# Whole-tile loads of k and v and a four-quadrant k-by-v product, in an attention and feed-forward kernel

## Chip, cores, metric

The kernel runs on one core of a Trainium2 chip. The metric is the device time of one execution in us; the trace of one profiled execution is read beside it. A ratio of two kernels is the mean time of one's fast runs over the mean of the other's fast runs of the same rounds, so it is not quite the ratio of the medians that are quoted.

In the profiles PE is TensorE, PEld its weight loads, DVE VectorE, ACT ScalarE, POOL GpSimd, and SP the engine whose queue issues most loads. The tiles kv_ps, o_ps, h_ and o_ hold k by v, q by kv, and the two large products. A kv section is an unbroken run of k-by-v matmuls. TensorE at half clock is TensorE at a granted clock of 0.50.

## The reference, cut

```python
kv  = np.einsum('bhsd,bhse->bhde', k, v)         # q, k, v: (8, 8, 576, 64) float32
out = np.einsum('bhsd,bhde->bhse', q, kv)
rms = np.sqrt(np.mean(out * out, axis=-1, keepdims=True) + 1e-06)
x   = (out / rms * g_norm).transpose(0, 2, 1, 3).reshape(4608, 512)
h   = x @ w_in                                    # 512 x 2048
y   = np.maximum(0.01 * h, h) @ w_out             # 2048 x 512
```

## The kernel before

The 4608 tokens are worked off in nine blocks of 512. Block 0 also rounds the weights, which arrive as float64, on ACT and DVE. Blocks 1 to 8 do the two large products by Strassen's scheme (tiles h_a to h_c and o_a to o_c). The attention of the next batch is cut into steps that are slipped between these products. The parts that the change touches, for batches 1 to 7:

```python
def load_rows(eng, src, t):                       # two heads, in two pieces of 64 rows
    pin(eng.dma_start(t[:64], src[:, :SLO, :].rearrange("h (p j) d -> p h j d", j=JJ)))   # j = 5
    pin(eng.dma_start(t[64:, :, :J], src[:, SLO:, :].rearrange("h (p j) d -> p h j d", j=J)))  # 4
...
def load_pair(b, p):                              # k, v, then q in four pieces, all on SP's queue
...
def attention_kv(b, p, kv_ps):                    # one pair of heads: two column tiles of 64
    k_in, v_in = k_ins.pop((b, p)), v_ins.pop((b, p))
    for j in range(JJ):
        n = P if j < J else 64
        for l in range(2):
            matmul(kv_ps[64 * l:64 * l + 64, p, :], lhsT=k_in[:n, l, j, :],
                   rhs=v_in[:n, l, j, :], start=(j == 0), stop=(j == JJ - 1))
...
def attention(b):
    ...
    for p in range(NP):                           # four pairs, one step each
        q_in = q_ins.pop((b, p))
        nc.vector.transpose(...)                  # q to qT
        attention_kv(b, p, kv_ps)
        nxt = (b, p + 2) if p + 2 < NP else (b + 1, p + 2 - NP)
        if nxt[0] < B:
            load_pair(*nxt)                       # k, v, q have two buffers each
        yield
    copy_kv(b, slice(0, NP), kv_ps)
    yield
    ...                                           # q by kv (o_ps), norm
```

Batch 0 has its own start: its loads go out first on two queues, TensorE transposes q, and "warm-keeping" matmuls on zeros (the program's name for them; the granted clock was 1.00 up to 29.95 us) stand between its sections, three of them between the four kv sections.

## Time and profile before

| | before |
|---|---|
| time, median of 4 runs of the first comparison | 1001.1 us |
| span of the profiled run | 996.7 us |
| first h_ps of block 0 | 31.35 us |
| start of block 1 (first h_a) | 158.84 us |
| first o_ps of batches 2, 3, 4, 7 | 185.3, 292.1, 397.8, 715.0 us |

The tables of this document give starts in us from the begin of the span. A row of a timeline has start, length, engine, line, operation, tiles, shape and count; the bracket gives idle time before it and what ended that. The prediction shows the rows of before.

### The profile page before, as it was taken

How to read it: one execution, taken by the hardware profiler on the slowest of the kernel's cores; microseconds unless marked ns; L12 is line 12 of the kernel's file. 1: busy time of each engine (PE TensorE's matmuls, PEld its weight loads, DVE VectorE, ACT ScalarE, POOL GpSimd, SP SyncE). 2: the span in 40 equal slices, each digit the busy share in tenths (PEclk: the TensorE clock that was granted, in tenths of full speed). 3: DMA queues.
4: the chain of work that ended last, by engine and by line, in shares of the span. 5: the costliest groups of instructions: out<-in, count | busy, mean ns of one | idle time of the engine just before them, and what ended most of it. 6: DMA issues, size and time to landing. Idle time of an engine off the chain costs nothing.

```text
span 996.7 us, 13085 instructions
## 1 busy us (share of the span) xinstructions
PE 970.3 (97%) x5130; PEld 766.5 (77%) x5130; DVE 435.6 (44%) x682; ACT 268.1 (27%) x531; POOL 500.7 (50%) x395
## 2 busy tenths in 40 slices
PE   9799999999999999999999999999999999999997
PEld 4444446778887888888887888788878888888885
DVE  1967993264235533363335433553246321422223
ACT  2644442431123211421133113311242122112210
POOL 1000213656655665556556665566556666666642
PEclk9799999999999999999999999999999999999999
DMA  9979904400340016000620043004100010001001
GB/s 208 224 177 246 232 15 117 115 2 0 95 137 1 1 52 178 2 1 0 175 58 1 1 128 103 2 0 95 43 1 1 1 43 1 1 1 43 0 1 43
DMA packets 45948, 63.41 MB, mean 64 GB/s; under 512 B 5952, under 2 KB 39744, under 8 KB 45888
## 3 DMA queue, kind: packets, MB, share of 16 engines
q1 hardware_dynamic: 35328, 51.96, 21.1%
q10 hardware_dynamic: 10432, 10.62, 3.4%
q8 instruction: 41, 0.67, 0.3%
q14 instruction: 19, 0.16, 0.1%
q0 software_dynamic: 128, 0.00, 0.0%
HBM read 53.12 MB, written 9.44 MB: 63 GB/s over the span
## 4 chain that ended last, share of the span: by engine, by line
PE 83%; DVE 4%; DMA 2%; SPq 1%; ACT 1%; issue 1%; DVEq 0%
PE o_a L87 21%; PE h_a L87 21%; PE h_c L87 11%; PE o_c L87 11%; PE o_b L87 6%; PE h_b L87 6%; PE o_acc L87 2%; PE kv_ps L87 2%; PE h_ps L87 2%; PE o_ps L87 2%; DVE qT L320 1%; DVE sum L282 1%; DMA v_in<-in_v_dram 1%; DMA k_in<-in_k_dram 1%; DVE g L388 0%
## 5 line engine op out<-in xcount | busy, mean ns | idle before, releaser
L388 DVE TENSOR_TENSOR o<-o_a,o 128x512 f32<-128x512 f32 x104 | 71.5, 688 | 132.8 <-PE o_a L87 132.8
L87 PE MATMUL o_a<-wt,gs 128*128 128x256 f32 x512 | 122.6, 382 | 0.0
L388 POOL TENSOR_TENSOR ws<-w 128x512 f32<-128x512 f32 x32 | 44.4, 1389 | 132.6 <-PE h_a L87 94.5
L388 POOL TENSOR_TENSOR wt<-w,w 128x512 f32<-128x512 f32 x32 | 40.9, 1280 | 139.0 <-PE o_a L87 135.6
L87 PEld LDWEIGHTS o_a<-wt,gs 128*128 128x128 f32 x512 | 95.9, 190 | 15.3 <-issue 1.9
L467 ACT ACTIVATE g<-g 128x512 f32<-128x512 f32 x96 | 60.5, 630 | 165.3 <-DVE g L388 165.3
L388 POOL TENSOR_TENSOR ws<-w,w 128x512 f32<-128x512 f32 x32 | 42.2, 1319 | 110.2 <-ACT cut L192 109.4
L388 POOL TENSOR_TENSOR gs<-g,g 128x512 f32<-128x512 f32 x64 | 81.5, 1274 | 22.9 <-ACT g L467 22.5
L472 ACT COPY g<-h_a 128x512 f32<-128x512 f32 x32 | 18.8, 586 | 251.0 <-PE h_a L87 239.1
L388 POOL TENSOR_TENSOR wt<-w,wt 128x512 f32<-128x512 f32 x64 | 83.9, 1310 | 2.5
L388 POOL TENSOR_TENSOR wt<-w 128x512 f32<-128x512 f32 x32 | 41.5, 1297 | 64.2 <-PE o_a L87 64.2
L87 PE MATMUL h_a<-xt,w 128*128 128x256 f32 x256 | 61.2, 382 | 7.8 <-DVE g L388 7.8
L87 PE MATMUL h_ps<-xT,w 128*128 128x512 f32 (+1 forms) x136 | 62.1, 605 | 6.6 <-DVE xT L301 4.5
L388 DVE TENSOR_TENSOR g<-h_b,g 128x512 f32<-128x512 f32 x32 | 22.1, 690 | 95.5 <-PE h_b L87 95.5
L388 DVE TENSOR_TENSOR o<-o_c,o 128x512 f32<-128x512 f32 x56 | 38.4, 685 | 56.8 <-PE o_c L87 56.8
L87 PE MATMUL o_a<-wt,g 128*128 128x256 f32 x256 | 60.8, 380 | 1.9 <-DVE o L388 1.9
L87 PE MATMUL h_a<-xT,ws 128*128 128x256 f32 x256 | 62.4, 386 | 0.0
L87 PE MATMUL h_a<-xt,ws 128*128 128x256 f32 x256 | 61.7, 384 | 0.0
L87 PE MATMUL o_a<-w,g 128*128 128x256 f32 x256 | 60.6, 379 | 0.8 <-DVE o L388 0.8
L87 PEld LDWEIGHTS h_a<-xt,w 128*128 128x128 f32 x256 | 48.1, 190 | 16.9 <-DVE g L388 10.6
L388 DVE TENSOR_TENSOR g<-h_c,g 128x512 f32<-128x512 f32 x32 | 22.1, 692 | 88.9 <-PE h_c L87 88.9
L87 PE MATMUL h_a<-xT,w 128*128 128x256 f32 x256 | 60.6, 379 | 0.0
(86 smaller groups left out, 1797.6 us busy)
## 6 DMA issues: line engine op xcount, KB each, us to landing
out_dram<-o ACTq DMA_DIRECT2D x36, 256.0 KB, 2.2
raw<-in_moe_w_in_dram SPq DMA_DIRECT2D x64, 128.0 KB, 5.0
raw<-in_moe_w_out_dram SPq DMA_DIRECT2D x16, 512.0 KB, 5.7
q_in<-in_q_dram SPq DMA_DIRECT2D x56, 144.0 KB, 3.5
q_in<-in_q_dram SPq DMA_DIRECT2D x56, 140.0 KB, 3.5
k_in<-in_k_dram SPq DMA_DIRECT2D x30, 160.0 KB, 3.7
v_in<-in_v_dram SPq DMA_DIRECT2D x30, 160.0 KB, 3.8
k_in<-in_k_dram SPq DMA_DIRECT2D x30, 128.0 KB, 3.7
```

What stands on the lines that cost most here:

```text
L87: pin(nc.tensor.matmul(*args, **kw))
L282: nc.vector.tensor_add(sums[l], sums[l], sq)
L320: nc.vector.transpose(qT[:, p, :].rearrange("p (t s) -> p s t", s=T), q_in.rearrange("p (s d) -> p s d", d=D)[:, :, :32])
L388: eng.tensor_tensor(out_, a, b_, op=ALU.subtract if minus else ALU.add)
L467: nc.scalar.activation(t, t if src is None else src, func=AF.Prelu, alpha=SLOPE)
L472: nc.scalar.copy(g11, bank)
```

## The change

It has three intents: load k, v and batch 0's q in one transfer per two heads, nine tokens per partition; multiply four heads at once in the four 64x64 quarters of TensorE; and so halve the number of kv sections, from four to two per batch.

```diff
-    def load_rows(eng, src, t):
-        pin(eng.dma_start(t[:64], src[:, :SLO, :].rearrange("h (p j) d -> p h j d", j=JJ)))
-        pin(eng.dma_start(t[64:, :, :J],
-                          src[:, SLO:, :].rearrange("h (p j) d -> p h j d", j=J)))
+    def half_of(p, i):
+        return i ^ (p & 1)
+
+    def load_two(eng, src, t):
+        pin(eng.dma_start(t.rearrange("p j d -> p (j d)"),
+                          src.rearrange("h (p j) d -> (h p) (j d)", j=J)))      # J = 9
...
+        for way, to, src, ts, p in (
+                ("a", q_ins, q, qs, 0), ("s", q_ins, q, qs, 1), ("a", q_ins, q, qs, 2),
+                ("s", q_ins, q, qs, 3), ("a", k_ins, k, ks, 0), ("s", v_ins, v, vs, 0),
+                ("a", k_ins, k, ks, 1), ("s", v_ins, v, vs, 1), ("s", k_ins, k, ks, 2),
+                ("s", v_ins, v, vs, 2), ("s", k_ins, k, ks, 3), ("s", v_ins, v, vs, 3)):
...
-    def attention_kv(b, p, kv_ps):
+    def attention_kv(b, m, kv_ps):
+        two = [(k_ins.pop((b, p)), v_ins.pop((b, p)), p) for p in (2 * m, 2 * m + 1)]
+        for j in range(J):
+            for i in range(2):
+                for k_in, v_in, p in two:
+                    r, c = 64 * i, 64 * half_of(p, i)
+                    matmul(kv_ps[p % 2][c:c + 64, m, :], lhsT=k_in[r:r + 64, j, :],
+                           rhs=v_in[r:r + 64, j, :], start=(j == 0), stop=(j == J - 1))
...
-            attention_kv(b, p, kv_ps)
-            nxt = (b, p + 2) if p + 2 < NP else (b + 1, p + 2 - NP)
-            if nxt[0] < B:
-                load_pair(*nxt)
+            if p % 2 == 0:
+                yield
+                continue
+            attention_kv(b, p // 2, kv_ps)
+            for i in (p - 1, p):
+                nxt = (b, i + 2) if i + 2 < NP else (b + 1, i + 2 - NP)
+                if nxt[0] < B:
+                    load_pair(*nxt)
             yield
...   (q transposes of batch 0 in 64x64 quarters, two kv tiles, one warm-keeping matmul
...    between the two kv sections of batch 0 in place of three between four)
```

More of the change, by code (lines that the diff above doesn't have):

```diff
@@ L59 @@
     NP = H // 2
-    J, JJ = 4, 5
-    SLO = 64 * JJ
+    J = S // 64
     T = S // 32
@@ L69 @@
     EPS = 1e-6
-    assert H * D == DM and S == 64 * (J + JJ) and 2 * E == D and NP * E == P and B * S == NB * NT
+    assert H * D == DM and S == 64 * J and D == 64 and 2 * E == D and H == 8 and NP * E == P and B * S == NB * NT
     assert DM // 2 == N2 and NE == 4
@@ L90 @@
     k_ins, v_ins, q_ins = {}, {}, {}
-    def load_rows(eng, src, t):
-        pin(eng.dma_start(t[:64], src[:, :SLO, :].rearrange("h (p j) d -> p h j d", j=JJ)))
-        pin(eng.dma_start(t[64:, :, :J],
-                          src[:, SLO:, :].rearrange("h (p j) d -> p h j d", j=J)))
+    def half_of(p, i):
[3 more added lines that the diff above has]
+                          src.rearrange("h (p j) d -> (h p) (j d)", j=J)))
         return t
     def in_tile(name):
-        return ins.tile([P, 2, JJ, D], F32, tag=f"{name}_in", name=f"{name}_in")
+        return ins.tile([P, J, D], F32, tag=f"{name}_in", name=f"{name}_in")
     def load_pair(b, p):
-        hs = slice(2 * p, 2 * p + 2)
-        k_ins[b, p] = load_rows(nc.sync, k[b, hs], in_tile("k"))
-        v_ins[b, p] = load_rows(nc.sync, v[b, hs], in_tile("v"))
+        k_ins[b, p] = load_two(nc.sync, k[b, 2 * p:2 * p + 2], in_tile("k"))
+        v_ins[b, p] = load_two(nc.sync, v[b, 2 * p:2 * p + 2], in_tile("v"))
         t = ins.tile([P, T * D], F32, tag="q_in", name="q_in")
@@ L111, in load_pair @@
                 r0, n = 64 * l + 32 * c, T * D - 32 * c
-                src = q[b, 2 * p + l].rearrange("(t s) d -> t (s d)", s=T)
+                src = q[b, 2 * p + half_of(p, l)].rearrange("(t s) d -> t (s d)", s=T)
                 pin(nc.sync.dma_start(t[r0:r0 + 32, :n], src[:, 32 * c:]))
@@ L118, in load_first @@
         early = xpool.tile([P, NE * NT], F32, tag="xT", name="early")
-        n = 2 * JJ * D
+        n = J * D
         def rows(t):
-            return t[:, :n].rearrange("p (l j d) -> p l j d", l=2, j=JJ)
+            return t[:, :n].rearrange("p (j d) -> p j d", j=J)
         ks, vs = ([in_tile(name) for _ in range(2)] for name in ("k", "v"))
@@ L129, in load_first @@
                   for j, t in ((0, ks), (2, vs)))
-        for src, to, ts, ways in ((q, q_ins, qs, "aass"), (k, k_ins, ks, "sssa"),
-                                  (v, v_ins, vs, "sssa")):
-            for p in range(NP):
-                to[0, p] = (ways[p], src[0, 2 * p:2 * p + 2], ts[p])
-        for to, p in ((q_ins, 0), (q_ins, 2), (q_ins, 1), (q_ins, 3),
-                      *((to, p) for p in range(NP) for to in (k_ins, v_ins))):
-            way, src, t = to[0, p]
-            to[0, p] = load_rows(nc.scalar if way == "a" else nc.sync, src, t)
+        for way, to, src, ts, p in (
[3 more added lines that the diff above has]
+                ("s", v_ins, v, vs, 2), ("s", k_ins, k, ks, 3), ("s", v_ins, v, vs, 3)):
+            to[0, p] = load_two(nc.scalar if way == "a" else nc.sync,
+                                src[0, 2 * p:2 * p + 2], ts[p])
     kvs = [consts.tile([P, NP, D], F32, name=f"kv_{i}") for i in range(2)]
@@ L244, with copy_kv, kv_tiles @@
     qTs = {}
-    def attention_kv(b, p, kv_ps):
-        k_in, v_in = k_ins.pop((b, p)), v_ins.pop((b, p))
-        for j in range(JJ):
-            n = P if j < J else 64
-            for l in range(2):
-                matmul(kv_ps[64 * l:64 * l + 64, p, :], lhsT=k_in[:n, l, j, :],
-                       rhs=v_in[:n, l, j, :], start=(j == 0), stop=(j == JJ - 1))
-    def copy_kv(b, ps, kv_ps):
-        nc.vector.tensor_copy(kvs[b % 2][:, ps, :], kv_ps[:, ps, :])
+    def attention_kv(b, m, kv_ps):
[6 more added lines that the diff above has]
+                           rhs=v_in[r:r + 64, j, :], start=(j == 0), stop=(j == J - 1))
+    def copy_kv(b, kv_ps):
+        for i in range(2):
+            nc.vector.tensor_copy(kvs[b % 2][:, i::2, :], kv_ps[i])
+    def kv_tiles():
+        return [ps_att.tile([P, NP // 2, D], F32, tag="att", name="kv_ps") for _ in range(2)]
     def t2k(n, name):
@@ L271, in outputs @@
                 r = slice(64 * l, 64 * l + 64)
-                matmul(o_ps[l][E * p:E * p + E, :], lhsT=kvs[b % 2][r, p, E * e:E * e + E],
+                matmul(o_ps[half_of(p, l)][E * p:E * p + E, :], lhsT=kvs[b % 2][r, p, E * e:E * e + E],
                        rhs=qTs[b][r, p, lo - b * S:hi - b * S], start=True, stop=True)
@@ L316, in attention @@
         qT = qTs[b] = work.tile([P, NP, S], F32, tag="qT", name="qT")
-        kv_ps = ps_att.tile([P, NP, D], F32, tag="att", name="kv_ps")
+        kv_ps = kv_tiles()
         for p in range(NP):
@@ L322, in attention @@
                 q_in.rearrange("p (s d) -> p s d", d=D)[:, :, :32])
-            attention_kv(b, p, kv_ps)
-            nxt = (b, p + 2) if p + 2 < NP else (b + 1, p + 2 - NP)
-            if nxt[0] < B:
-                load_pair(*nxt)
+            if p % 2 == 0:
[6 more added lines that the diff above has]
+                    load_pair(*nxt)
             yield
-        copy_kv(b, slice(0, NP), kv_ps)
+        copy_kv(b, kv_ps)
         yield
@@ L343, in first_attention @@
         qT = qTs[0] = work.tile([P, NP, S], F32, tag="qT", name="qT")
-        kv_ps = ps_att.tile([P, NP, D], F32, tag="att", name="kv_ps")
-        rest = ps_m.tile([P, NP, 64], F32, tag="oc", name="rest_ps")
+        kv_ps = kv_tiles()
+        rest = [ps_m.tile([P, NP // 2, 64], F32, tag=t, name="rest_ps") for t in ("oc", "oa")]
         for j in range(3):
@@ L349, in first_attention @@
             q_in = q_ins.pop((0, p))
-            q_ps = ps_m.tile([P, J, P], F32, tag=("ha", "hb", "hc", "oa")[p], name="q_ps")
-            for j in range(JJ):
-                n = P if j < J else 64
+            q_ps = ps_m.tile([P, J - 1, 64], F32, tag=("ha", "hb", "hc", "ha")[p], name="q_ps")
+            for j in range(J):
                 for l in range(2):
-                    to = (q_ps[:, j, :] if j < J else rest[:, p, :])[64 * l:64 * l + 64]
-                    matmul(to, lhsT=q_in[:n, l, j, :], rhs=ident[:n, :n], start=True, stop=True)
+                    r, c = slice(64 * l, 64 * l + 64), 64 * half_of(p, l)
+                    matmul((q_ps[:, j, :] if j < J - 1 else rest[p % 2][:, p // 2, :])[c:c + 64],
+                           lhsT=q_in[r, j, :], rhs=ident[r, r], start=True, stop=True)
             keep_warm()
-            for r, c0, step in ((0, 0, JJ), (64, SLO, J)):
-                to = qT[:, p, c0:c0 + 64 * step].rearrange("p (t j) -> p j t", j=step)
-                (nc.vector.tensor_copy if r else nc.scalar.copy)(
-                    to[:, :J, :], q_ps[:, :, r:r + 64])
-        nc.vector.tensor_copy(
-            qT[:, :, :SLO].rearrange("p a (t j) -> p a t j", j=JJ)[:, :, :, J], rest)
-        for p in range(NP):
-            attention_kv(0, p, kv_ps)
-            if p < NP - 1:
+            to = qT[:, p, :].rearrange("p (t j) -> p j t", j=J)
+            h = J // 2
+            nc.scalar.copy(to[:, :h, :], q_ps[:, :h, :])
+            nc.vector.tensor_copy(to[:, h:J - 1, :], q_ps[:, h:, :])
+        for i in range(2):
+            nc.vector.tensor_copy(
+                qT.rearrange("p a (t j) -> p a t j", j=J)[:, i::2, :, J - 1], rest[i])
+        for m in range(2):
+            attention_kv(0, m, kv_ps)
+            if m == 0:
                 keep_warm()
-            copy_kv(0, slice(p, p + 1), kv_ps)
+        copy_kv(0, kv_ps)
         for j in range(3, 7):
```

## The prediction

> **What bounds the kernel now.** I read the page first: busy shares, then the chain that ended last.
>
> ```profile
> PE 970.3 (97%) x5130; PEld 766.5 (77%) x5130; DVE 435.6 (44%) x682; ACT 268.1 (27%) x531; POOL 500.7 (50%) x395
> ...
> PE 83%; DVE 4%; DMA 2%; SPq 1%; ACT 1%; issue 1%; DVEq 0%
> PE o_a L87 21%; PE h_a L87 21%; PE h_c L87 11%; PE o_c L87 11%; PE o_b L87 6%; PE h_b L87 6%; PE o_acc L87 2%; PE kv_ps L87 2%; PE h_ps L87 2%; PE o_ps L87 2%; DVE qT L320 1%; DVE sum L282 1%; DMA v_in<-in_v_dram 1%; DMA k_in<-in_k_dram 1%; DVE g L388 0%
> ```
>
> TensorE is the bound. What the change touches (kv_ps) is 2% of the chain, some 20 us; that caps the main gain. Next the tile view of kv_ps and TensorE's timeline around batch 2's four sections.
>
> ```profile
> L87 PEld LDWEIGHTS kv_ps<-v_in,k_in x600: 129/138/138, 16.9 to 702.5; 128*64 128x64 f32 x120, 64*64 64x64 f32 x30
> L87 PE MATMUL kv_ps<-v_in,k_in x600: 218/222/270, 16.9 to 702.6; 128*64 128x64 f32 x120, 64*64 64x64 f32 x30
> ```
> ```profile
> 172.30 1.99 PE L87 MATMUL h_a<-xt,w 128*128 128x256 f32 x8 [0.78 <-DVE g L388]
> 174.22 0.95 PE L87 MATMUL kv_ps<-v_in,k_in 128*64 128x64 f32 x20
> 175.61 0.95 PE L87 MATMUL kv_ps<-v_in,k_in 128*64 128x64 f32 x20 [0.45 <-DMA v_in<-in_v_dram]
> 176.49 1.99 PE L87 MATMUL h_a<-xT,w 128*128 128x256 f32 x8
> 178.32 1.03 PE L87 MATMUL h_c<-xt,ws 128*128 128x256 f32 x4
> ```
>
> The reader should see that one pair is 20 matmul records (ten calls, two passes each), that 175.61 to 176.49 is 0.88 us for it, and that the h_a section after it takes 1.83 us to the next start, where sections away from a kv section take 1.73 (8 x 216 ns). The records one by one show why: two column tiles start 7 ns apart; the first round lasts 107 ns, further rounds 58 ns; then 150 ns pass at the switch to the fifth token group (64 rows) and 147 ns at the switch back. So 0.107+6x0.058+0.150+0.107+0.147 = 0.87 us. The drain before the section costs about 0.09 and the refill after it 0.107: **1.07 us per pair**, 4.27 per batch.
>
> The start is different: there a chain of loads, ACT and DVE decides.
>
> ```profile
> 22.73 0.95 PE L87 MATMUL kv_ps<-early_kv 128*64 128x64 f32 x20
> 23.61 3.21 PE L87 MATMUL o_ps<-qT,kv 64*32 64x256 f32 x64
> 31.35 2.05 PE L87 MATMUL h_ps<-xT,w 128*128 128x256 f32 x4 [4.53 <-DVE xT L301]
> ```
> ```profile
> 22.85 0.68 ACT L190 ACTIVATE add<-raw 128x512 uint32<-128x512 uint32 x1 [6.50 <-DMA raw<-in_moe_w_in_dram]
> 23.44 0.65 ACT L192 ACTIVATE cut<-raw 128x512 f32<-128x512 f32 x1
> 24.72 0.38 ACT L276 ACTIVATE sum<-o_ps 128x256 f32<-128x256 f32 x1 [0.63 <-PE o_ps L87]
> ```
>
> ACT first waits for the first weight rows, behind all of q, k, v in the queue, then for o_ps. And block 0's end is DVE-bound, as this row of the windows view says (columns: length; busy of PE, PEld, DVE, ACT, POOL; clock; DMA share; GB/s):
>
> ```profile
> 96.00:154.00 58.00, 54.83 (x201) 22.95 (x200) 52.82 (x83) 26.49 (x54) 11.88 (x8) 1.00 0.52 121
> ```
>
> DVE is busy 52.8 of 58 us, and at 146.7 and 151.9 PE waits 0.78 and 1.48 us for DVE's rounded weights.
>
> [...] about 150 ns at each switch, including the last matmul; and o_ps, in eight 64x32 tiles, does 16 passes of 192 columns in 0.48 us. [...] In the loaded first 20 us, packets of 1024 and 1280 B took about 80 and 99 ns (12.9 B/ns), those of 4096 B some 210 ns a little later (19 B/ns): larger is better here.
>
> **The change part by part.**
> *kv products, batches 1 to 7.* Two pairs become one section: 36 calls, 72 passes, 18 rounds of four quadrants. If quadrants overlap as column tiles do (four starts 7 ns apart fit in 58 ns): 0.107+16x0.058+0.147 = 1.18 us, plus 0.09+0.107 at the edges = 1.38; two per batch 2.76 against 4.27. **1.5 us saved per batch** where PE is the bound.
>
> *Loads.* One whole-tile load replaces two, for k and v. An issue took 0.60 us in the SP timeline whether of 160 or 128 KB, both 128 rows, so a pair's k and v cost 1.3 us of issue instead of 2.6. But the loads of both next pairs now come after the second step:
>
> ```profile
> 167.75 1.93 SPq L113 DMA_DIRECT2D q_in<-in_q_dram x4
> 169.78 0.60 SPq L94 DMA_DIRECT2D k_in<-in_k_dram x1
> 170.43 0.60 SPq L95 DMA_DIRECT2D k_in<-in_k_dram x1
> 171.07 0.60 SPq L94 DMA_DIRECT2D v_in<-in_v_dram x1
> 171.72 0.61 SPq L95 DMA_DIRECT2D v_in<-in_v_dram x1
> ```
>
> Let X be the start of the first double section. Loads start at X+1.3 (the section, then the release). k, v of the third pair 1.3, its q 2.0, k of the fourth 0.65: its v is issued at X+5.3 and, with 3.7 us to landing (the median of v loads), lands at X+9.0. In block 1 there is no o product yet between the steps, so the second double section is due after 1.38+2x1.73 plus the 0.78 wait for DVE: X+5.6. **A stall of 3.3 us in batch 2**, in place of the 0.45. From batch 3 on five products lie between steps two and three and two more before step four (264.7, 274.4, 278.9 before): due about X+14, hidden. DVE's transpose of the third pair's q wants its q at about X+9, landing X+8: just hidden.
>
> *Start.* q, k, v of batch 0 are 3.54 MB; the last v landed at 20.3 us by the trace's landing events. My choice: packets of 2304 B carry 10% more per time, so it lands near 18.7, and the first weights near 21.1 instead of 22.75. On PE the four kv sections with three warm-keeping fillers (16.93 to 23.61) become two with one: 1.2+1.1+1.2, ready at 20.4; the copies of kv now all follow it (+0.6). So o_ps comes at 21.1, ACT finishes the first weights at 22.4, and the Squares start there instead of at 24.72: **2.3 us earlier**, and the rest of the start with them. The q transposes for batch 0 change from 1.28 to about 1.2 us per pair: nothing.
>
> *Block 0.* The first sections of batch 1 give 0.7 us before DVE becomes the bound at 96; the rest of that batch's 1.5 is lost to DVE. So block 0 ends 3.0 us earlier.
>
> Sum: -3.0 (start and block 0), batch 2 -1.5-0.45+3.3 = +1.4, five batches x -1.5 = -7.5: about -9 us, **991 us** from 1000.1.
>
> **Rivals.** (1) *Quadrants do not overlap*[...]. Then 36 rounds: 2.2 us a section, 2.4 with edges, 4.9 per batch against 4.27; the main gain turns into about +0.6 x 6 and the time is near 1001. [...] against it, eight tiles overlap in o_ps. (2) *The load is hidden or the SP order is kinder*: no stall in batch 2, 987 to 988. Against it: the pair before was already 0.45 us late although its load started a step earlier. (3) *The stall lets the clock drop*: in the 30 to 40 us slice the granted clock was 0.50 after PE's 4.5 us idle. A 3.3 us stall could cost up to 3 us more: 994. Against it: 2.1 us at 218 did no such thing. (4) *The new transfers are much better at the start*: at most 2.5 us more, 988, as DVE and ACT then bound it. (5) DVE becomes the bound in the main blocks through late q: it has slack there (311 of 790 us busy), so only single stalls.
>
> **Range and chances.** All gains together without any loss (start 5, eight batches at 1.5, the two DMA waits 1.4) make 18 us, 982: below the 2% line of 980 hardly anything leads. No overlap plus a clock drop makes 1004 or so. I take 985 to 998. Faster by over 2%: 0.04; within 2%: 0.94; slower: 0.02.
>
> **What would show it.** kv sections of 72 records lasting about 1.2 us, 58 ns per round of four: step one right; 2 us and more: rival 1. A wait of about 3 us on a v_in load before the second kv section of batch 2 (near 172 us), none in later batches. The first h_ps at about 29 instead of 31.35 us, block 1 starting near 156 instead of 158.84. A gap of PE waiting for DVE's weights at the end of block 0 somewhat longer than before, since DVE ends it. Wrong it would be if DVE's order of work changes much, or if waits appear in every block.

-3.0 + 1.4 - 7.5 is -9.1, about -9 us, and so 991 from 1000.1. "Drain" and "refill" are names for what the records of before show: the last pass before the section at 174.22 took 0.309 us to the next start instead of 0.216, and the first one after the section at 175.61 took 0.320. Two figures are estimates: that packets of 2304 B carry 10% more per time, chosen between the 12.9 B/ns of the smaller packets and the 19 B/ns of those of 4096 B; and the up to 3 us of rival 3, for which before had one stretch of half clock to go by, 29.95 to 40.19 us, with TensorE idle for 4.53 us up to 31.35.

## The result

The changed kernel took 990.5 us (median of 4 runs, 988.5 to 993.6) against 1001.1 us: ratio 0.990, interval 0.986 to 0.993. Measured again later, beside other kernels, it took 992.5 us (6 runs) against 998.7 us, ratio 0.993. The gain is 6 to 11 us.

The page of the changed kernel, busy shares and the lines of the chain:

```profile
PE 958.0 (97%) x5702; PEld 763.8 (77%) x5702; DVE 435.3 (44%) x688; ACT 268.1 (27%) x531; POOL 499.0 (50%) x395
...
PE h_a L86 22%; PE o_a L86 21%; PE h_c L86 11%; PE o_c L86 11%; PE h_b L86 6%; PE o_b L86 6%; PE o_acc L86 5%; PE h_ps L86 5%; PE kv_ps L86 2%; PE o_ps L86 2%; DVE qT L327 1%; DVE sum L289 1%; DMA k_in<-in_k_dram 1%; DMA v_in<-in_v_dram 1%; DMA raw<-in_moe_w_in_dram 1%
```

TensorE is still the bound, and the share of busy time says nothing of what happened inside. The starts of the stages do:

| stage, by the two profiled runs | before | after | moved by |
|---|---|---|---|
| first h_ps | 31.35 | 26.57 | -4.8 |
| block 1 starts | 158.84 | 151.19 | -7.7 |
| first o_ps of batch 2 | 185.3 | 184.7 | -0.6 |
| of batch 3 | 292.1 | 291.7 | -0.4 |
| of batch 4 | 397.8 | 395.9 | -1.9 |
| of batch 7 | 715.0 | 708.7 | -6.3 |
| end | 996.7 | 990.2 | -6.6 |

Almost all of the 7.7 us won by the start of block 1 is gone some 33 us later. From batch 4 on each batch gives 1.5 us. These are single traces, and their starts scatter: in a second trace of the changed kernel (e11_after_again) the first h_ps came at 26.40 and block 1 at 152.78, and in e6_before_late_loads, which starts like before, they came at 32.79 and 159.76. So 1.5 us between two starts can be chance. The place of the loss, in TensorE's timeline of the changed kernel:

```profile
163.90 1.99 PE L86 MATMUL h_a<-xt,w 128*128 128x256 f32 x8 [0.78 <-DVE g L400]
166.96 0.29 PE L86 MATMUL kv_ps<-v_in,k_in 64*64 64x64 f32 x2 [1.06 <-DMA v_in<-in_v_dram]
172.31 2.19 PE L86 MATMUL kv_ps<-v_in,k_in 64*64 64x64 f32 x70 [5.06 <-DMA v_in<-in_v_dram]
174.43 3.45 PE L86 MATMUL h_a<-xT,w 128*128 128x256 f32 x8
177.72 1.03 PE L86 MATMUL h_c<-xt,ws 128*128 128x256 f32 x4
```

TensorE waits 1.06 us for the third pair's v and 5.06 us for the fourth's, where before it waited 0.45. And then the rest of the section takes 2.12 us to the next start and the h section 3.29, where 1.21 and 1.83 are usual. The windows view (columns as in the prediction; the granted clock stands behind POOL) shows a lower clock there:

```profile
166.00:174.00 8.00, 1.98 (x66) 1.91 (x69) 1.26 (x1) 0.53 (x1) 3.43 (x3) 0.79 0.83 184
174.00:180.00 6.00, 6.00 (x37) 5.03 (x31) 1.65 (x3) 0.93 (x2) 0.00 (x0) 0.71 0.74 209
```

The clock events of the trace put half clock at 170.6 to 177.4 us. In the same windows of before the clock was 1.00. A second stretch of half clock, 3.4 us long, follows a wait of 2.12 us at 217.9; that wait is in both kernels, the drop is not, and it took the 1.5 us that batch 3 should have given.

The loads of that section, in the timeline of SP's queue:

```profile
161.24 0.33 SPq L98 DMA_DIRECT2D k_in<-in_k_dram  x1
161.62 1.14 SPq L98 DMA_DIRECT2D v_in<-in_v_dram  x1
162.85 1.77 SPq L115 DMA_DIRECT2D q_in<-in_q_dram  x4
164.72 0.37 SPq L98 DMA_DIRECT2D k_in<-in_k_dram  x1
165.13 0.43 SPq L98 DMA_DIRECT2D v_in<-in_v_dram  x1
```

The section started at 159.92; the last v was issued at 165.13, and by the landing events it landed at 172.18, 7 us later. The start, in TensorE's and ACT's timelines:

```profile
17.10 1.28 PE L86 MATMUL kv_ps<-early_kv 64*64 64x64 f32 x72
18.87 2.92 PE L86 MATMUL o_ps<-qT,kv 64*32 64x256 f32 x64 [0.49 <-DVE kv L259]
26.57 0.76 PE L86 MATMUL h_ps<-xT,w 128*128 128x256 f32 x1 [4.78 <-DVE xT L308]
```
```profile
18.13 0.66 ACT L191 ACTIVATE add<-raw 128x512 uint32<-128x512 uint32 x1 [3.73 <-DMA raw<-in_moe_w_in_dram]
```

A section of 72 passes takes 1.21 us from its start to TensorE's next start. The first weights are there at 18.1 us instead of 22.85, and o_ps follows at 18.9 instead of 23.6.

### The profile page after: what moved, and what is told of

Read it like the earlier page. It is cut to its first block, busy times and chain, and to the rows that moved or that the text cites. A ratio compares the mean times of both kernels' runs of the same rounds, so it can differ in the third digit from the quotient of the medians.

```text
span 990.2 us, 14098 instructions
## 1 busy us (share of the span) xinstructions
PE 958.0 (97%) x5702; PEld 763.8 (77%) x5702; DVE 435.3 (44%) x688; ACT 268.1 (27%) x531; POOL 499.0 (50%) x395
## 4 chain that ended last, share of the span: by engine, by line
PE 90%; DVE 6%; DMA 2%; ACT 1%; issue 1%; SPq 0%; ACTq 0%; DVEq 0%
PE h_a L86 22%; PE o_a L86 21%; PE h_c L86 11%; PE o_c L86 11%; PE h_b L86 6%; PE o_b L86 6%; PE o_acc L86 5%; PE h_ps L86 5%; PE kv_ps L86 2%; PE o_ps L86 2%; DVE qT L327 1%; DVE sum L289 1%; DMA k_in<-in_k_dram 1%; DMA v_in<-in_v_dram 1%; DMA raw<-in_moe_w_in_dram 1%
## 5 line engine op out<-in xcount | busy, mean ns | idle before, releaser
L86 PE MATMUL o_c<-wt,gs 128*128 128x256 f32 x256 | 60.8, 381 | 0.0
```

Of the source, the lines that this page charges most:

```text
L86: pin(nc.tensor.matmul(*args, **kw))
```

## The experiments

My theory after the traces: (a) the four quadrants overlap, 1.5 us per batch; (b) the start wins 4.8 us, by quicker loads and a shorter chain of sections; (c) batch 2 loses some 7 us to v arriving late and to the slow clock after that wait. Rivals: for (a), that halving the number of sections is all; for (b), that only the new order of queues counts; for (c), that whole-tile transfers land slowly by themselves. Times are medians; ratios are to the kernel before of the same rounds.

| run | time us | ratio (95% interval) |
|---|---|---|
| e1_early_loads | 988.8 | 0.989 (0.986 to 0.992) |
| e2_diagonal | 1006.7 | 1.0065 (1.005 to 1.008) |
| e3_split_loads | 993.0 | 0.993 (0.992 to 0.995) |
| e4_fillers | 989.8 | 0.990 (0.988 to 0.991) |
| e5_kv_early_q_late | 987.6 | 0.987 (0.986 to 0.989) |
| e6_before_late_loads | 998.2 | 0.998 (0.997 to 1.000) |
| e7_old_queues | 992.2 | 0.992 (0.990 to 0.994) |
| e8_q_last | 989.9 | 0.990 (0.988 to 0.991) |
| e9_before_paired | 1003.9 | 1.005 (1.004 to 1.007) |
| e10_mixed | 986.2 | 0.987 (0.986 to 0.989) |
| e11_after_again | 992.5 | 0.993 (0.992 to 0.995) |

All gave right results.

### Do four quadrants overlap? (e2_diagonal)

```diff
     def half_of(p, i):
-        return i ^ (p & 1)
+        return i
```

> The changed kernel, with the heads of odd pairs not swapped, so that both pairs of a section use the same two quadrants and the other two stand idle. Loads, steps and switches are unchanged. Theory (four quadrants overlap): a section of 72 passes goes from 1.21 us to 36 rounds of 58 ns, about 2.2 to 2.3 us, and the time rises by 16 x 1.05 = about 15 us less what the batch 2 wait and the start hide, say 12 to 15, to 1003 to 1006. Rival (the gain is only that there are half as many sections and mode switches): sections stay at about 1.2 us and the time at 990.

One section, in TensorE's timeline:

```profile
268.52 2.36 PE L86 MATMUL kv_ps<-v_in,k_in 64*64 64x64 f32 x72
270.81 1.56 PE L86 MATMUL h_a<-xT,ws 128*128 128x256 f32 x6
```

It lasts 2.29 us instead of 1.21, with the same number of passes, sections and switches. So the overlap of all four quadrants is what pays: with two, the change would be slower than the kernel before, 1006.7 against 1000.3 us. The time lies just above the expected 1003 to 1006. (a) stands and its rival falls.

### The start (e3_split_loads, e7_old_queues)

```diff
-        pin(eng.dma_start(t.rearrange("p j d -> p (j d)"),
-                          src.rearrange("h (p j) d -> (h p) (j d)", j=J)))
+        cut = (J + 1) // 2
+        rows = src.rearrange("h (p j) d -> (h p) (j d)", j=J)
+        flat = t.rearrange("p j d -> p (j d)")
+        pin(eng.dma_start(flat[:, :cut * D], rows[:, :cut * D]))
+        pin(eng.dma_start(flat[:, cut * D:], rows[:, cut * D:]))
```

> The changed kernel, with each whole-tile load cut into two of 1280 and 1024 B a row, in the same order and on the same queues. Theory (the start gained 4.8 us because packets of 2304 B take about 95 ns under load, hardly more than those of 1024 to 1280 B): the first weights land at 21 to 23 us instead of 18, the first h_ps starts at 29 to 31 instead of 26.6, and block 1 starts about 3 to 4 us later. Rival (the order of the queues and the two fillers fewer gave it): the first h_ps stays within 1 us of 26.6. The wait in batch 2 should hardly change, as the bytes ahead of the last v are the same.

ACT's timeline, its first work on weights:

```profile
21.53 0.66 ACT L194 ACTIVATE add<-raw 128x512 uint32<-128x512 uint32 x1 [6.89 <-DMA raw<-in_moe_w_in_dram]
```

The first weights landed at 21.4 us instead of 18.0, the first h_ps started at 29.95 instead of 26.57, and block 1 at 154.65 instead of 151.19. Cutting the transfers gave back 3.4 us of the 4.8, and the 3.4 us passed on whole to block 1. The wait in batch 2 was 4.06 us instead of 6.12, which I had not expected.

But my mechanism, the packet size, was not right. By the packet records, packets of 1024 and 1280 B took 80 and 99 ns before and 46 and 55 ns here (medians, 5 to 10 us), though they have the same sizes. What differs is the shape: before, one transfer filled 64 partitions with two heads; here it fills all 128. The engines were also far from full here, a busy share of 0.66 in 5 to 10 us against 1.08 before, and the rate was no higher, 220 against 215 GB/s. In all four kernels whose starts I listed there are never more than eight transfers in flight (the four of 0.2 KB on POOL's queue not counted), and mostly the next is issued at the moment an earlier one lands. With whole tiles, eight transfers carry twice the bytes: 341 GB/s in 10 to 15 us, against 223 with cut ones. That this limit is what cost the 3.4 us is argued from these lists, not shown by a run, and neither is whether it lies in the chip or in the program.

```diff
-                ("a", q_ins, q, qs, 0), ("s", q_ins, q, qs, 1), ("a", q_ins, q, qs, 2),
-                ("s", q_ins, q, qs, 3), ("a", k_ins, k, ks, 0), ("s", v_ins, v, vs, 0),
-                ("a", k_ins, k, ks, 1), ...
+                ("a", q_ins, q, qs, 0), ("s", q_ins, q, qs, 2), ("a", q_ins, q, qs, 1),
+                ("s", q_ins, q, qs, 3), ("s", k_ins, k, ks, 0), ("s", v_ins, v, vs, 0),
+                ("s", k_ins, k, ks, 1), ...
```

> The changed kernel with the queues and the order of the first loads as before (q of pairs 0 and 1 on ACT's queue, k and v of pairs 0 to 2 all on SP's, the last pair on ACT's). Theory (packets make most of the start's gain, splitting them cost 3.4 of 4.8 us): the first h_ps starts within 1.4 us of 26.6 and the time is 990 to 992. Rival (order and queues matter as much): the first h_ps comes at 29 or later.

The first h_ps came at 27.98 us, 1.4 later, and the first weights at 19.3; the time lies just above the expected 990 to 992. In the seven traces that start like the changed kernel (after, e1, e4, e5, e8, e10, e11) the first h_ps came at 26.4 to 27.5, so part or most of the 1.4 us may be chance. Order and queues count less than whole transfers; that they count at all is not shown. The two numbers must not be added as shares: the start needs both the weights and o_ps. In e2_diagonal the weights were there at 18.2, but o_ps came at 21.3 after the longer sections, and the first h_ps at 28.8.

### Batch 2: when the loads start (e1_early_loads)

A third buffer for k and v lets each pair's loads go out at its own step again; four output buffers instead of six make the room.

```diff
-        return ins.tile([P, J, D], F32, tag=f"{name}_in", name=f"{name}_in")
+        return ins.tile([P, J, D], F32, tag=f"{name}_in", name=f"{name}_in", bufs=3)
...
-            if p % 2 == 0:
-                yield
-                continue
-            attention_kv(b, p // 2, kv_ps)
-            for i in (p - 1, p):
-                nxt = ...
+            if p % 2:
+                attention_kv(b, p // 2, kv_ps)
+            nxt = (b, p + 2) if p + 2 < NP else (b + 1, p + 2 - NP)
+            if nxt[0] < B:
+                load_pair(*nxt)
             yield
```

> The changed kernel, with a third k and a third v buffer (paid for with four output buffers instead of six), so that each pair's loads start at its own step again and not two pairs at once after the second step. Theory: batch 2's wait of 1.06 + 5.06 us and the slow clock after it (about 2.4 us) come from when the loads start. They then shrink to 1 us or less, the o_ps of batch 2 comes near 178 us instead of 184.7, and the time falls by 6 to 9 us to about 983. Rival (whole-tile transfers land slowly whenever they start): a wait of several us stays, and the time stays within 2 us of 990.

TensorE's timeline, the second section of batch 2 and the h section after it:

```profile
167.43 1.27 PE L86 MATMUL kv_ps<-v_in,k_in 64*64 64x64 f32 x70 [0.44 <-DMA v_in<-in_v_dram]
168.63 1.99 PE L86 MATMUL h_a<-xT,w 128*128 128x256 f32 x8
```

The wait shrank to 0.44 us, the clock stayed up, and the first o_ps of batch 2 came at 177.5 us instead of 184.7. So (c) stands and its rival falls, for these are the same whole-tile transfers. But the time fell by only about 2 us, not 6 to 9. The gain was lost from batch 4 on, in a new wait of 0.74, 1.19 and 1.33 us in three later blocks. DVE's timeline before the second of these:

```profile
533.00 1.22 DVE L327 STREAM_TRANSPOSE qT<-q_in 128x576 f32<-128x576 f32 x1
534.07 1.45 DVE L308 TENSOR_TENSOR xT<-xT,inv 128x768 f32<-128x768 f32 x1
535.44 0.68 DVE L397 TENSOR_TENSOR o<-o_a,o 128x512 f32<-128x512 f32 x1
```

The build chooses the order of those DVE instructions that the program does not pin. With q loaded earlier it put a transpose of q ahead of an output addition that TensorE waits for. In the changed kernel that transpose is absent there, and the addition starts 1.47 us after the last transpose of inv (538.79 to 540.26) instead of 2.92 us. That the earlier q brought this order is tested by e5_kv_early_q_late below.

### Bytes ahead of the last v (e8_q_last), and what starts a load (e6_before_late_loads)

```diff
-            for i in (p - 1, p):
-                nxt = (b, i + 2) if i + 2 < NP else (b + 1, i + 2 - NP)
-                if nxt[0] < B:
-                    load_pair(*nxt)
+            for part in (load_kv, load_q):
+                for i in (p - 1, p):
+                    nxt = (b, i + 2) if i + 2 < NP else (b + 1, i + 2 - NP)
+                    if nxt[0] < B:
+                        part(*nxt)
```

> The changed kernel, with the loads after the second and fourth step in the order k, v, k, v, q, q instead of k, v, q, k, v, q; no more buffers. Theory (bytes ahead of the last v decide): 1.18 MB instead of 1.73 MB stand before it, so it lands about 8.5 us after the start of the first double section instead of 12.3, the wait in batch 2 shrinks from 6.1 to about 3 us, and the time falls by 2 to 5 us, to 985 to 988. Rival (the landing takes a fixed latency after issue): v is issued 2 us earlier and the wait is 4 us.

```profile
170.07 1.49 PE L86 MATMUL kv_ps<-v_in,k_in 64*64 64x64 f32 x70 [1.80 <-DMA v_in<-in_v_dram]
```

TensorE's timeline shows a wait of 1.80 us, less than the expected 3. The section began at 162.03 and the last v landed at 169.94, after 7.9 us instead of 12.3: 1.18 MB in 6.6 us from the first load, against 1.76 MB in 10.9 us for the changed kernel, and 10.4 us for before. In all three it is a rate of 160 to 180 GB/s, not a fixed latency after the last v's issue, for from that issue it took 4.4, 7.0 and 3.8 us. The time, 989.9, missed the expected 985 to 988. DVE's order changed here too: at the end of block 0 TensorE waited 2.64 and 1.60 us for weights, and in batch 2 o_ps waited 1.22 us for a transpose of q. That q had landed at 174.9; its transpose stood behind an addition in DVE's order and ran at 182.5.

For the kernel before, I first moved only the place of the loads in the program:

```diff
-            nxt = (b, p + 2) if p + 2 < NP else (b + 1, p + 2 - NP)
-            if nxt[0] < B:
-                load_pair(*nxt)
+            for i in (p - 1, p) if p % 2 else ():
+                nxt = (b, i + 2) if i + 2 < NP else (b + 1, i + 2 - NP)
+                if nxt[0] < B:
+                    load_pair(*nxt)
```

> The kernel before with one part of the change alone: the loads of both next pairs are issued after the second and fourth pair instead of after each. Theory (what delays v in batch 2 is the amount of data that has to follow once the second section is over, k, v and q of one pair and k and v of the next, 1.73 MB in 10.4 to 10.9 us in both kernels): the last v lands near 180 us, the wait before the fourth section grows from 0.45 to 4 to 5 us, and with a slow clock after it the time is 1004 to 1007. Rival (whole-tile transfers are what lands late): the wait stays under 1 us and the time at 1000.

```profile
166.02 0.60 SPq L94 DMA_DIRECT2D k_in<-in_k_dram  x1
```

This expectation failed, and usefully. SP's timeline has the third pair's k issued at 166.02, just after the first pair's section (165.03 to 165.9), and before the second's at 169.6. So this load did not start where it stands in the program; it started 0.12 us after the section that freed its buffer had ended. The wait was 0.17 us and the time that of before.

### Pairing alone (e9_before_paired)

So the buffers have to come free later, by putting the products of two pairs in one step of the kernel before:

```diff
-            attention_kv(b, p, kv_ps)
-            nxt = ...
+            if p % 2 == 0:
+                yield
+                continue
+            for i in (p - 1, p):
+                attention_kv(b, i, kv_ps)
+            for i in (p - 1, p):
+                nxt = (b, i + 2) if i + 2 < NP else (b + 1, i + 2 - NP)
+                if nxt[0] < B:
+                    load_pair(*nxt)
```

> The kernel before with the products of two pairs in one step, as in the change, but with its own two column tiles, its own loads in two pieces, and the loads of both next pairs after them. The last experiment on this failed: moving only the place of the loads in the program changed nothing, as a load starts when its buffer comes free, and the first pair's buffers still came free one step early. Here they come free together. Theory: pairing the products is what delays the loads; the wait in batch 2 grows from 0.45 to 4 to 6 us, with a slow clock after it, and the time is 1003 to 1008. Rival (it needs the whole-tile transfers): the wait stays under 1.5 us and the time under 1001.

```profile
179.15 1.53 PE L87 MATMUL kv_ps<-v_in,k_in 128*64 128x64 f32 x20 [4.57 <-DMA v_in<-in_v_dram]
180.61 3.22 PE L87 MATMUL h_a<-xT,w 128*128 128x256 f32 x8
```

TensorE's timeline has the loss of batch 2 without whole-tile loads or quadrants: a wait of 4.57 us, and an h section of 3.06 us to the next start (183.67) instead of 1.83. The kernel is 5.2 us slower than before. The pairing, which frees both pairs' buffers at once and late, is the cause.

### The clock (e4_fillers)

```diff
+            if b == 2 and p == 3:
+                idle = ps_m.tile([P, NT], F32, tag="oc", name="idle_ps")
+                for _ in range(7):
+                    matmul(idle, lhsT=w1_sb[0][0][:, 0, 0, :], rhs=w2_sb[0][0][:, 0, :],
+                           start=True, stop=True)
             attention_kv(b, p // 2, kv_ps)
```

> The changed kernel, with seven matmuls of 512 columns (about 6 us) on data that is there, put before the second kv section of batch 2, where TensorE waits for v. Theory: after that wait the kv section and the next h section ran at half clock (2.12 and 3.29 us instead of 1.21 and 1.83). With the wait filled they run at 1.21 and 1.83, and the time falls by about 2 us. Rival (the slow sections come from data that arrives late, not from the clock): they stay long. Time: 988 to 989, hardly outside the noise, so the trace decides.

```profile
166.91 6.17 PE L86 MATMUL idle_ps<-w,w 128*128 128x512 f32 x14
173.01 1.28 PE L86 MATMUL kv_ps<-v_in,k_in 64*64 64x64 f32 x72
174.22 1.99 PE L86 MATMUL h_a<-xT,w 128*128 128x256 f32 x8
176.05 1.89 PE L86 MATMUL h_c<-xt,ws 128*128 128x256 f32 x8
```

With the wait filled, TensorE's timeline has the section at 1.21 us and the h section at 1.83. From the start of block 1 to batch 2's first o_ps it took 30.6 us instead of 33.5. So it was the wait of 6 us that brought the clock down here. The medians (989.8 against 990.5) cannot show 2 us; the trace does.

### A better version (e5_kv_early_q_late, e10_mixed, e11_after_again)

e5 keeps the early loads of k and v and leaves q after the second step:

```diff
+            after = [(b, i + 2) if i + 2 < NP else (b + 1, i + 2 - NP) for i in (p - 1, p)]
+            if after[1][0] < B:
+                load_kv(*after[1])
+            for nxt in after if p % 2 else ():
                 if nxt[0] < B:
-                    load_pair(*nxt)
+                    load_q(*nxt)
...   (third k and v buffers, four output buffers)
```

> As the first experiment (third k and v buffers, k and v loaded at each pair's own step), but q of both pairs is still loaded after the second step, behind k and v. In the first experiment batch 2 gained 7.2 us and blocks 4 to 7 lost 0.7 to 1.3 us each at a new wait of TensorE for DVE, with a transpose of q standing in DVE's queue ahead of an output addition. Theory: that order of DVE came from the earlier q loads; it goes back to that of the changed kernel in blocks 2 to 8, the new waits go, batch 2 keeps its gain, and the time is 982 to 985. Rival: the new waits come from the four output buffers, or from k and v loads; they stay, and the time is 987 to 989.

The new waits of later blocks went, each gave its 1.5 us, and the wait for v in batch 2 was 0.35 us, though o_ps waited 1.23 us there for a transpose of q, as in e8_q_last. The four output buffers are thereby cleared: they are in this kernel too. But block 1 began at 154.4 us instead of 151.2 to 152.8: DVE's order in block 0 was another, TensorE waited 2.65 us for weights at 142, and half clock lasted 10.2 us from 25.8 on instead of 6.8 from 23.8. At 987.6 the time missed the expected 982 to 985.

e10 takes q from the first experiment for the steps of batches 1 and 2, and from e5 for the rest (`for n in nxt[1:] if b <= 2 else nxt if p % 2 else ():`).

> Third k and v buffers, k and v at each pair's own step. q at its own step too for the steps of batches 1 and 2 (as in the first experiment, which lost nothing before 285 us), and after the second step from batch 3 on (as in the fifth, whose DVE order in blocks 3 to 8 is that of the changed kernel). Theory: the losses of both were DVE's order, in blocks 4 to 7 there and in block 0 here, and both go: first h_ps near 26.6 to 27, block 1 from 151 to 152, o_ps of batch 2 near 177.5, no new waits after 285, time 981 to 984. Rival: the new waits come with the buffers; time 986 to 988.

> The changed kernel unaltered, for its spread beside the one above on the same chip: 988 to 994, with the wait of about 6 us and the half clock in batch 2 again. If the half clock after the 2.1 us wait near 218 us is a matter of chance, it may be absent in this trace.

e10 took 986.2 us and the changed kernel, in the same rounds, 992.5; the two ratios, 0.9873 and 0.9933, put e10 0.6% ahead. e5 has the same ratio in its own rounds, 0.9873, so which of the two is better is open. The time falls into the range of e10's rival, but not for its reason: no new waits came after 285 us. Block 1 began at 154.1, though, not at 151 to 152, and the time is 2 us above the expected range: in this trace half clock at the start again lasted 10.2 us, and the second section of batch 1 waited 1.04 us for v.

e11 repeats the 6 us wait (6.02) and the half clock of 6.8 us in batch 2. The drop after the 2.1 us wait near 218 us is absent. Over the 13 traces, that wait, always 2.11 or 2.12 us, was followed by half clock in six. So about 1.7 us of a single trace is chance here.

## Why the prediction was right, and where it was not

- **The kv sections.** Predicted 1.18 us per section and 1.5 us per batch. Measured 1.21 us, and 5.9 us over batches 4 to 7. e2_diagonal shows that it is the overlap. Right. (The terms for a section of before add up to 0.86 us, not 0.87; nothing hangs on it.)
- **The start.** Predicted 2.3 us, measured 4.8. The mis-sized term is "packets of 2304 B carry 10% more per time": they took 93 to 96 ns, no longer than the 1280 B of before, and the first weights landed at 18.0 us, not 21.1. And the reason given, packet size, was not the reason: equal sizes took 46 and 55 ns in 128-row transfers. Rival 4, transfers much better at the start, came true with its full 2.5 us.
- **Block 0.** Predicted that DVE is the bound from 96 us and swallows most of batch 1's gain, so 3.0 us at block 1's start; measured 7.7. This step failed. A DVE that is busy 52.8 of 58 us had its inputs earlier and moved along: TensorE's waits for weights at the block's end are 1.15 and 1.47 us, against 0.78 and 1.48, and e3_split_loads passes a shift of 3.4 us on as 3.5. Batch 1 gave its 1.5 us, and the 0.91 us wait for v went as well (in e11 a wait of 1.43 us stood there again). Another 0.8 us came between the first h_ps and the first o_acc, 11.38 us instead of 12.14: half clock ended 4.0 us after the first h_ps, against 8.8. In e10, where it lasted 10.2 us again, the stretch took 12.27. Why it was shorter is not shown.

```profile
139.08 3.70 PE L86 MATMUL h_ps<-xT,w 128*128 128x512 f32 x8 [1.15 <-DVE w L200]
144.25 1.53 PE L86 MATMUL o_acc<-w,gT 128*128 128x512 f32 x3 [1.47 <-DVE w L200]
```

- **Batch 2.** The stall was predicted in the right place, for the right reason, in later loads. Its size was wrong: 3.3 us predicted, 6.1 measured. The issue of the last v came at X+5.2, as predicted (X+5.3), in part by luck: most issues took 0.33 to 0.43 us instead of the 0.60 assumed, but one of v took 1.14. The failed term is "3.7 us to landing": that is the median of single loads, where here 1.76 MB follow one another and arrive at 160 GB/s; it landed at X+12.3. Rival 3, the clock, came true and cost another 2.4 us or so, by the two slow sections.
- **Later batches.** No waits on v from batch 3 on, as predicted. Batch 3's gain went to the chance drop of the clock; in e11, without the drop, it took 105.3 us from batch 2's first o_ps to batch 3's, against 107.0 here and 106.8 before.

Sum, by the traces: start and block 0 -7.7 instead of -3.0; batch 2 +7.1 instead of +1.4; batch 3 +0.2 and batches 4 to 7 -5.9, instead of -7.5. The total of 991 us was met because two errors of about 5 us cancelled, and that is luck.

## What to carry to other kernels

Before merging steps, ask which buffers then come free later. Here the loads that refill them started that much later, whatever their place in the program (0.11 to 0.12 us after the section's end in the changed kernel and in e6_before_late_loads), and one more buffer each for k and v bought back about 6 us of waiting. When several loads follow one another, estimate the last one's landing from all the bytes ahead and the measured rate (160 to 180 GB/s here), not from a median latency (3.7 us, where it took 7.0). As block 0 shows, an engine that is 90% busy in a stage (DVE, 52.8 of 58 us) need not be its bound: when its inputs came earlier, it moved along with what feeds it.

## What the traces show of the hardware

- In the changed kernel both row halves of TensorE wrote each of the two kv_ps tiles at the same time, in different halves of its partitions, with right results and four passes per 58 ns round (section at 159.92). Both in the same half of one tile was not tried.
- At each change of the matmul's form about 150 ns passed after a matmul of 64 columns, that matmul included (147 to 152 ns in before and in the changed kernel, at full clock and without a wait), and the first round after it took 107 ns instead of 58.
- A wait of 2.1 us was followed by half clock in six of 13 traces, and so was one of 1.8 us in e8_q_last, while one of 2.64 us there was not. The stretches of half clock lasted 3.4, 6.8 or 10.2 us.
- Packets of 1024 and 1280 B took 80 and 99 ns in transfers to 64 partitions (before, 5 to 10 us), and 46 and 55 ns in transfers to all 128 (e3_split_loads, the same stretch).
- An issue took 0.60 us for a piece of 64 rows by two heads (k and v in before) and about 0.33 to 0.45 us for a whole load of two heads as 128 rows (the changed kernel), where nothing held it up.
